# Decode attention with a gated MLP: two merged Wo transfers, a quartered x load, and the stores' semaphores

## The chip, the cores and the metric

The kernel runs on one core of a Trainium2 chip. The metric is the device time of one execution in microseconds (us); lower is better. "TensorE", "VectorE", "ScalarE", "GpSimd" and "SyncE" are the core's engines; the profile calls them PE (PEld for its weight loads), DVE, ACT, POOL and SP, and writes SPq or ACTq for what their instruction queues do, such as issuing transfers.

## The reference

One token for each of B = 8 sequences, D = 512. All tensors are bf16.

```python
xn = layernorm(x)                                   # [8, 512]
q  = xn @ wq                                        # 512 x 4096: 32 heads of 128
k, v = last 2048 of the 8192 cached positions       # 8 kv heads, each for 4 q heads
p  = softmax(q k^T * 128**-0.5);   o = p v          # [8, 4096]
s  = o @ wo                                         # 4096 x 512
g  = silu((sigmoid(xn @ w_gate) * (xn @ w_up)) @ w_down)   # 512 -> 1792 -> 512
out = x + s * g
```

## The kernel before

**What is loaded.** Every large tensor is read once: Wq as one transfer of 4 MB, the keys as 8 of 4 MB, the values as 16 of 2 MB, gate and up as two of 1.8 MB, down as one of 1.8 MB, and Wo (`wo_sb`) as eight pieces. All of these are issued by SyncE through `load` (L110 to L113) and so stand in one queue; each spreads over 128 partitions. x (`x_bf`, L122) is one transfer of 8 rows of 1 KB, issued by ScalarE.

**What sets the order.** `loads` (L194 to L202) is a list written ahead: keys and values by due times, then gate/up, the last two values, down, and Wo last of all. `issue_loads` (L208) issues from it as long as the buffer that the next load needs has been released: three buffers for Wq, keys and weights (`kring`), four for values (`vring`). The engines' instruction order is the order in which the program is written (`manual_schedule`, L88).

**What is computed.** LayerNorm of x on VectorE (L236 to L249), its transpose on TensorE (L259), the q projection on Wq (L391). Then one loop over 116 slots (L654): VectorE transposes keys in place (`k_turn`, L450), TensorE forms scores (L465), softmax follows, and TensorE multiplies the values (`pv`, L599, and `pv_sum`, L619). Gate and up (`unit_in`, L341) and down (`unit_out`, `b_ps`, L367) are placed among them. The last product is Wo:

```python
    for k in range(KW):          # KW = 32; row block k of Wo is wo_parts[k]
        for c in range(NCOL):    # two column halves, side by side on TensorE
            nc.tensor.matmul(a_ps[32*c : 32*(c+1), :], lhsT=o2_sb[:, k, :],
                             rhs=wo_parts[k][:, DC*c : DC*(c+1)], ...)
```

So `a_ps` (L702) takes the blocks k = 0 to 31 in order, and each block waits for the piece of Wo that holds it. A piece of blocks t0 to t1 is one run of (t1 - t0) KB on each of the 128 partitions. After `a_ps` come two VectorE instructions (`prod`, L713, and `y_bf`, L715) and the two stores (L717), one from SyncE and one from ScalarE.

**Semaphores of transfers.** The compiler layer gives the transfers eight completion semaphores in turn, in the order of the program. A transfer whose semaphore was used before waits, on the issuing engine, until the earlier user has landed. There are 39 transfers; the stores have semaphores 5 and 6 (counted from 0). At the end of the kernel (L746) SyncE waits for the semaphores in ascending order.

Of the kernel before, what the change touches and what calls it, by code (L numbers as in the profile page):

```python
# [10 lines left out]
def kernel(  # L11
# [13 lines left out]
    nc = tc.nc  # L25
    P = 128
# [83 lines left out]
    def load(dst, src, q=None):  # L110
        if q is None:
            q = nc.sync
        q.dma_start(out=dst, in_=src)  # L113

    def k_tile(shape, name):
        return kring.tile(shape, bf16, name=name, tag="kring", align_bytes=ALIGN)
# [2 lines left out]
        return vring.tile(shape, bf16, name=name, tag="vring", align_bytes=ALIGN)  # L119

    x_bf = work.tile([B, D], bf16, name="x_bf")
    nc.scalar.dma_start(out=x_bf[:], in_=A_x.flatten_outer_dims())  # L122

    wq_sb = k_tile([P, KT, Hq * Dh], "wq_sb")
    load(wq_sb[:], A_wq.rearrange("(p kt) n -> p kt n", kt=KT))
# [49 lines left out]
    def load_wo():  # L175
        t = k_tile([P, KW, D], "wo_sb")
        for t0, t1 in (
            (0, 8),
            (8, 16),
            (16, 20),  # L180
            (20, 24),
            (24, 28),
            (28, 30),
            (30, 31),
            (31, 32),
        ):
            load(t[:, t0:t1, :], wo_view[:, t0:t1, :])
            for k in range(t0, t1):
                wo_parts[k] = t[:, k, :]
# [18 lines left out]
    def issue_loads():  # L208
        while loads_done[0] < len(loads):
            x = loads[loads_done[0]]  # L210
            kind, i = x
            order, n = (v_order, VRING) if kind == 1 else (k_order, KRING)
            at = order.index(x)
            if at >= n and order[at - n] not in released:
                break
            if kind == 0:
                load_k(i)
            elif kind == 1:
                load_v(i)
            else:  # L220
                (load_gate_up, load_down, load_wo)[i]()
            loads_done[0] += 1
# [22 lines left out]
        out=rstd[:], in_=mv[:, 1:2], func=AF.Sqrt, bias=eps_t[:], scale=1.0  # L245
# [4 lines left out]
        out=xn_bf[:],  # L250
# [7 lines left out]
    for kt in range(KT):  # L258
        nc.tensor.transpose(  # L259
            out=xnT_ps[:, kt, :], in_=xn_bf[:B, kt::KT], identity=ident[:B, :B]  # L260
        )
    x2_ps = psum1.tile([NCOL * 32, DC], f32, name="x2_ps", tag="misc")
    for c in range(NCOL):
# [23 lines left out]
        out=PermF[:], in_=ident[:].rearrange("m (h q r) -> m q h r", q=NQ, r=rep)  # L287
# [4 lines left out]
        out=Hm[:],  # L292
        in_=ident[:].rearrange("p (a gl) -> p gl a", gl=GL),
# [6 lines left out]
    for j in range(GL):  # L300
        for gg in range(NG):
            g = NG * gg + j // 2
            nc.vector.tensor_copy(
                out=spread[:, gg, j % 2, :, j], in_=ident[:, 32 * g : 32 * g + PP]
# [5 lines left out]
        out=rows_of[:],  # L310
        in_=ident[:].rearrange("p (a m) -> p m a", m=w),
# [5 lines left out]
        out=Sel[:], in_=rows_of[:].rearrange("p (g c r) -> p c g r", g=GL, c=NCH)  # L317
# [5 lines left out]
    for gg in range(NG):  # L323
        rows = slice(32 * gg, 32 * (gg + 1))
        cols = slice(NE * GL * rep * gg, NE * GL * rep * (gg + 1))
        for e in range(NE):
            nc.vector.tensor_copy(
                out=pick[rows, e, cols].rearrange("p (h d) -> p h d", d=NE)[:, :, e],
                in_=ident[rows, 32 * gg : 32 * gg + GL * rep],
# [386 lines left out]
    for c in range(NCOL):  # L716
        queues[c].dma_start(  # L717
            out=out.flatten_outer_dims()[:, DC * c : DC * (c + 1)],
            in_=y_bf[32 * c : 32 * c + B, :],
# [31 lines left out]
```

## Time and profile before

| | us |
|---|---|
| median of 3 runs (197.93 to 197.95) | 197.94 |
| the profiled execution | 198.09 |
| its span, first to last instruction | 196.3 |
| PE / DVE / ACT busy in it | 90.5 / 109.9 / 27.4 |

The 40 digits of the profile's second part show the 16 transfer engines (its DMA row) at 9 tenths or more in every slice but the first and the last. The profile's fourth part follows the chain of work that ended last; its fifth and the timeline give instructions with the idle time before them and what ended that idle time.

### The profile page before, as it was taken

To read this page: it belongs to the slowest core of one execution; us is meant where nothing else is said; L and a number is where in the kernel's file an instruction comes from. 1 tells how busy PE (TensorE), PEld (TensorE's weight loads), DVE (VectorE), ACT (ScalarE), POOL (GpSimd) and SP (SyncE) were. 2 spreads that over 40 slices of the span, in tenths; PEclk is the share of its full clock that TensorE was granted. 3 is DMA by queue.
4 is the path that set the end of the run, shared out by engine and by line. 5 is a ranking of instruction groups with operands and counts; after the bars stand their busy time and mean duration, and the time that the engine had idled before them with its cause. 6 is when DMAs were issued, how large, how long until landed. Compare 5 with 4: busy or idle time off the path is not lost.

```text
span 196.3 us, 2503 instructions
## 1 busy us (share of the span) xinstructions
PE 90.5 (46%) x1046; PEld 43.9 (22%) x1046; DVE 109.9 (56%) x176; ACT 27.4 (14%) x69; POOL 1.6 (1%) x8
## 2 busy tenths in 40 slices
PE   0134004434333158403664764963566653555682
PEld 0011001111001012100332431342333331233561
DVE  3606399999999998899969836143000000120301
ACT  3006050000000074000000051420000004000000
POOL 3000000000000000000000000000000000000000
PEclk9999999999999999955558797599555555555879
DMA  6999999999999999999999999999999999999990
GB/s 235 447 441 434 441 429 441 427 434 424 434 427 427 427 427 434 417 424 451 441 414 431 427 427 427 429 431 431 427 431 427 434 430 435 424 426 423 422 363 19
DMA packets 5243, 81.18 MB, mean 414 GB/s; under 512 B 600, under 2 KB 880, under 8 KB 1392
## 3 DMA queue, kind: packets, MB, share of 16 engines
q1 hardware_dynamic: 5200, 81.01, 96.7%
q8 instruction: 8, 0.13, 0.2%
q10 hardware_dynamic: 32, 0.01, 0.0%
q14 instruction: 3, 0.02, 0.0%
HBM read 81.01 MB, written 0.01 MB: 413 GB/s over the span
## 4 chain that ended last, share of the span: by engine, by line
DMA 59%; DVE 27%; PE 9%; issue 1%; SPq 1%; ACT 0%; ACTq 0%; DVEq 0%
DVE k_sb L450 22%; DMA k_sb<-in_A_k_cache_dram 20%; DMA v_sb<-in_A_v_cache_dram 15%; DMA wgu_sb<-in_B_w_up_dram 13%; DMA wo_sb<-in_A_wo_dram 12%; PE pT_ps L526 3%; PE acc_ps L599 3%; PE s_ps L465 2%; DVE pT_sb L545 2%; DVE mx L479 1%; DVE pt_bf L513 1%; PE a_ps L702 1%; SPq L113 1%; PE den_ps L574 1%; PE o_ps L619 0%
## 5 line engine op out<-in xcount | busy, mean ns | idle before, releaser
L450 DVE STREAM_TRANSPOSE k_sb<-k_sb 128x1024 f32<-128x1024 f32 x64 | 73.9, 1208 | 5.7 <-DMA k_sb<-in_A_k_cache_dram 5.7
L465 PE MATMUL s_ps<-k_sb,qz_sb 128*32 128x512 bf16 x256 | 33.3, 585 | 56.5 <-DVE k_sb L450 50.7
L599 PE MATMUL acc_ps<-v_sb,pT_sb 128*32 128x256 bf16 x512 | 31.4, 367 | 17.4 <-DMA v_sb<-in_A_v_cache_dram 17.4
L628 DVE TENSOR_SCALAR o_sb<-o_ps,rden 16x128 bf16<-16x128 f32 x16 | 5.4, 336 | 46.3 <-PE o_ps L619 46.2
L465 PEld LDWEIGHTS <-qz_sb 128*32 128x32 bf16 x256 | 10.3, 121 | 73.8 <-issue 53.2
L599 PEld LDWEIGHTS <-pT_sb 128*32 128x32 bf16 x512 | 17.9, 121 | 28.9 <-DMA v_sb<-in_A_v_cache_dram 21.3
L610 ACT COPY acc_sb<-acc_ps 128x256 f32<-128x256 f32 x16 | 6.0, 373 | 81.1 <-PE acc_ps L599 81.1
L619 PE MATMUL o_ps<-acc_sb,Sel 128*16 128x128 f32 x64 | 14.1, 362 | 6.9 <-ACT acc_sb L610 6.9
L619 PEld LDWEIGHTS o_ps<-acc_sb,Sel 128*16 128x16 f32 x64 | 6.6, 118 | 13.9 <-ACT acc_sb L610 11.5
L526 PE MATMUL pT_ps<-pt_bf,spread 128*128 128x512 bf16 x16 | 7.5, 622 | 0.9 <-DVE pt_bf L513 0.7
L545 DVE TENSOR_SCALAR pT_sb<-pc_bf,Hm 128x1024 bf16<-128x1024 bf16 x16 | 6.6, 475 | 1.1 <-PE acc_ps L599 1.1
L391 PE MATMUL q_ps<-wq_sb,xnT_sb 128*32 128x512 bf16 x32 | 3.6, 629 | 7.5 <-DMA wq_sb<-in_A_wq_dram 7.5
L493 ACT ACT_TABLE_LOAD x1 | 1.3, 1283 | 39.4 <-DVE nm L487 39.4
L513 DVE STREAM_TRANSPOSE pt_bf<-p_bf 128x512 bf16<-128x512 bf16 x8 | 4.9, 674 | 2.2 <-ACT p_bf L493 2.2
L702 PE MATMUL a_ps<-wo_sb,o_sb 128*32 128x256 bf16 x64 | 5.7, 324 | 0.9 <-DMA wo_sb<-in_A_wo_dram 0.8
L534 ACT CAST pc_bf<-pT_ps 128x512 bf16<-128x512 f32 x8 | 4.6, 586 | 9.4 <-PE pT_ps L526 6.6
L422 ACT COPY qz_sb<-qT_sb 32x32 bf16<-32x32 bf16 x20 | 4.8, 241 | 7.7 <-DVE qT_sb L410 7.5
L479 DVE TENSOR_REDUCE mx<-s_ps 128x1 f32<-128x512 f32 x8 | 5.3, 659 | 1.0 <-PE acc_ps L599 1.0
L341 PE MATMUL d_ps<-wgu_sb,xnT_sb 128*32 128x448 bf16 x32 | 3.4, 573 | 4.9 <-DMA wgu_sb<-in_B_w_up_dram 2.5
L493 ACT ACTIVATE p_bf<-s_ps,nm 128x512 bf16<-128x512 f32 x8 | 5.4, 685 | 0.5 <-DVE nm L487 0.5
L410 DVE STREAM_TRANSPOSE qT_sb<-q_sb 128x512 bf16<-128x512 bf16 x2 | 1.4, 690 | 7.1 <-ACT q_sb L405 7.1
L702 PEld LDWEIGHTS <-o_sb 128*32 128x32 bf16 x64 | 4.4, 117 | 2.3 <-issue 1.9
(59 smaller groups left out, 37.2 us busy)
## 6 DMA issues: line engine op xcount, KB each, us to landing
k_sb<-in_A_k_cache_dram SPq DMA_DIRECT2D x8, 4096.0 KB, 21.8
v_sb<-in_A_v_cache_dram SPq DMA_DIRECT2D x16, 2048.0 KB, 18.5
wq_sb<-in_A_wq_dram SPq DMA_DIRECT2D x1, 4096.0 KB, 12.4
wo_sb<-in_A_wo_dram SPq DMA_DIRECT2D x2, 1024.0 KB
wgu_sb<-in_B_w_gate_dram SPq DMA_DIRECT2D x1, 1792.0 KB
wgu_sb<-in_B_w_up_dram SPq DMA_DIRECT2D x1, 1792.0 KB, 24.7
wd_sb<-in_B_w_down_dram SPq DMA_DIRECT2D x1, 1792.0 KB, 29.7
wo_sb<-in_A_wo_dram SPq DMA_DIRECT2D x3, 512.0 KB, 25.6
```

The source lines that it names most:

```text
L450: nc.vector.transpose(out=kw, in_=kw)
L465: nc.tensor.matmul(s_tiles[i][32 * g : 32 * (g + 1), :], lhsT=qz_sb[:, hb, h, 2 * a + e, :], rhs=kT[:, :, a, h, :, e], start=(n == 0), sto ...
L479: nc.vector.reduce_max(out=mx_of[hb][:, kq : kq + 1], in_=s_tiles[i][:], axis=AX.X)
L493: nc.scalar.activation(out=p_bf[:, :, kq], in_=s_tiles.pop(NK * hb + kq)[:].rearrange("p (o c j) -> p c j o", o=2, j=NC), func=AF.Exp, bia ...
L513: nc.vector.transpose(out=pt[:, w * n : w * (n + 1)], in_=p_bf[:, w * n : w * (n + 1)])
L526: nc.tensor.matmul(pT_ps[:], lhsT=spread[:, gg, y].rearrange("p k g -> p (k g)"), rhs=pt[:, c, y, :], start=(y == 0), stop=(y == 1), skip_ ...
L545: nc.vector.tensor_scalar(out=pT_of[hb, gg][:, :, gl, :], in0=pc, scalar1=Hm[:, gl : gl + 1], scalar2=None, op0=ALU.mult,)
L599: nc.tensor.matmul(acc_tiles[i][w * c : w * (c + 1), :], lhsT=pT[:, GL * rep * ch : GL * rep * ch + w], rhs=v_tiles[i][:, ch : ch + NCH, : ...
L610: nc.scalar.copy(out=acc_sb[:], in_=acc_tiles.pop(i)[:])
L619: nc.tensor.matmul(o_ps[rows, :], lhsT=Sel[:, c].rearrange("p g r -> p (g r)"), rhs=acc_sb[:, Dh * c : Dh * (c + 1)], start=(c == 0), stop ...
L628: nc.vector.tensor_scalar(out=o_sb[rows, b, :], in0=o_ps[rows, :], scalar1=rden_of[b // NQ][rows, b % NQ : b % NQ + 1], scalar2=None, op0= ...
L702: nc.tensor.matmul(a_ps[32 * c : 32 * (c + 1), :], lhsT=o2_sb[:, k, :], rhs=wo_parts[k][:, DC * c : DC * (c + 1)], start=(k == 0), stop=(k ...
```

## The change

The load of x becomes four transfers, one for each quarter of its columns (8 rows of 256 bytes each), still on ScalarE's queue. In Wo's list of pieces, blocks 0 to 16 become one transfer of 16 KB runs and blocks 16 to 24 one of 8 KB runs; the last four pieces (24 to 28, 28 to 30, 30 to 31, 31 to 32) are as before. There are then 40 transfers (three more for x, two fewer for Wo), and the stores come to semaphores 6 and 7, the last of the eight.

```diff
-    nc.scalar.dma_start(out=x_bf[:], in_=A_x.flatten_outer_dims())
+    for c in range(4):
+        nc.scalar.dma_start(
+            out=x_bf[:, P * c : P * (c + 1)],
+            in_=A_x.flatten_outer_dims()[:, P * c : P * (c + 1)],
+        )
...
     def load_wo():
         t = k_tile([P, KW, D], "wo_sb")
         for t0, t1 in (
-            (0, 8),
-            (8, 16),
-            (16, 20),
-            (20, 24),
+            (0, 16),
+            (16, 24),
             (24, 28),
             (28, 30),
             (30, 31),
```

No instruction of another engine is added, removed or moved. Waits move: the blocks 0 to 7 of `a_ps` now wait for the whole first half of Wo, and blocks 16 to 19 for the whole quarter 16 to 24. On SyncE, two issues of Wo go; each piece of Wo still waits for the transfer eight places before it, which for the last piece is now a value tile and was the down weights. Some key and value loads also wait for a quarter of x, whose semaphore they take over.

## The prediction

> **What bounds the kernel now.** I read the page first, for the transfer engines.
>
> ```profile
> DMA  6999999999999999999999999999999999999990
> GB/s 235 447 441 434 441 429 441 427 434 424 434 427 427 427 427 434 417 424 451 441 414 431 427 427 427 429 431 431 427 431 427 434 430 435 424 426 423 422 363 19
> DMA packets 5243, 81.18 MB, mean 414 GB/s; under 512 B 600, under 2 KB 880, under 8 KB 1392
> q1 hardware_dynamic: 5200, 81.01, 96.7%
> ```
>
> All 16 transfer engines are busy from the first slice to the last but one, with no dip. The 5200 packets of q1, SyncE's queue, are 36 loads of 128 rows plus 16 marks each, plus 16 for one store; the 600 below 512 bytes are 36 x 16 + 3 x 8, the marks of all 39 transfers. So a load costs each of the 16 engines eight rows and one mark. Next, SyncE's issues of loads:
>
> ```profile
> DMA to landing us min/median/max: 10.0/21.7/31.1
> L113 SPq DMA_DIRECT2D wo_sb<-in_A_wo_dram x8: 327/328/422, 153.5 to 182.6; - x8
> ```
>
> A load is issued at least 10.0 us before it lands: the queue always holds more work, and an issue or a wait on SyncE costs nothing until it is delayed by about that much. What counts is what the stream of loads has to move, and what comes after its last byte. That is in the chain of waits (start, duration, what) and in the timeline:
>
> ```profile
> 168.56 22.62 DMA wo_sb<-in_A_wo_dram
> 191.22 0.61 PE a_ps L702 x8
> 192.27 0.29 PE a_ps L702 x2
> 192.60 0.30 PE a_ps L702 x2
> 192.92 0.42 DVE prod L713
> 193.37 0.28 DVE y_bf L715
> ```
>
> ```profile
> 178.37 1.90 PE L599 MATMUL acc_ps<-v_sb,pT_sb 128*32 128x256 bf16 x32 [1.46 <-DMA v_sb<-in_A_v_cache_dram]
> 180.80 1.03 PE L619 MATMUL o_ps<-acc_sb,Sel 128*16 128x128 f32 x4 [0.54 <-ACT acc_sb L610]
> 184.22 2.25 PE L367 MATMUL b_ps<-wd_sb,hT_sb 128*32 128x256 bf16 x28 [1.36 <-DVE o_sb L649]
> 186.23 3.55 PE L702 MATMUL a_ps<-wo_sb,o_sb 128*32 128x256 bf16 x40
> 190.01 0.61 PE L702 MATMUL a_ps<-wo_sb,o_sb 128*32 128x256 bf16 x8 [0.24 <-DMA wo_sb<-in_A_wo_dram]
> 191.22 1.66 PE L702 MATMUL a_ps<-wo_sb,o_sb 128*32 128x256 bf16 x16 [0.60 <-DMA wo_sb<-in_A_wo_dram]
> ```
>
> TensorE takes blocks 0 to 19 of Wo (40 matmuls, two a block) without a stop, then waits for each later piece: blocks 24 to 27 land at about 191.2, the last at about 192.6, and the last pair ends at 192.90. The end is set by the landing of the last pieces, and the rest follows in fixed steps.
>
> **The change part by part.** *Fewer rows on the wire.* Windows of stages with different row lengths (their last number is GB/s):
>
> ```profile
> 30.00:80.00 50.00, 22.11 (x179) 6.78 (x168) 48.20 (x53) 6.41 (x13) 0.00 (x0) 1.00 1.00 432
> 120.00:160.00 40.00, 23.61 (x312) 12.16 (x312) 7.78 (x22) 5.22 (x12) 0.00 (x0) 0.63 1.01 430
> 181.00:186.00 5.00, 3.21 (x34) 2.42 (x34) 1.61 (x2) 0.00 (x0) 0.00 (x0) 0.84 1.01 426
> 186.00:189.00 3.00, 3.00 (x36) 2.62 (x32) 0.41 (x1) 0.38 (x1) 0.00 (x0) 0.56 1.01 408
> ```
>
> They are mostly rows of 32 KB, of 16 KB, of 8 KB, and of 4 KB with some of 8 KB. One engine moves a 32 KB row at 432/16 = 27.0 bytes/ns. An 8 KB row at 426/16 = 26.6 takes 308 ns against 303 at that rate; a 4 KB row at 408/16 = 25.5 takes 161 against 152. So a row costs 4 to 9 ns beyond its bytes. The change removes 256 rows, 16 on each engine, and two marks: 16 x 4 to 16 x 9 gives 0.06 to 0.14 us. I take 0.09, nearer the 8 KB window, which is the longer and purer of the two. It all lies ahead of the last landing: a gain of 0.09.
>
> The Trainium skill has a rule by which this would be much more: "DMA: Bandwidth & Descriptors", section "Anatomy of one DMA", gives each transfer a fixed cost of about 2.0 us besides its bytes. Two transfers fewer in the stream would then be an estimated 4 us less. The windows above contradict that for a full queue: the stream does not stop between transfers.
>
> *Issues and waits on SyncE.* Two issues of 0.33 us go, and each remaining piece waits for an earlier landing than before (the last for a value tile, not for the down weights). With a lead of 10.0 us, this is worth nothing, and nor are the waits on x's semaphores that some key loads gain: x has landed long before.
>
> *The first block waits longer.* Block 0 of `a_ps` now needs the whole first half. In the trace it started at 186.23. When did blocks 8 to 15 land? Blocks 20 to 23 landed just before 190.01; blocks 16 to 23 are 1.05 MB, at 408 GB/s 2.57 us, so the first half is there at 187.40, 187.35 with the gain above. TensorE starts the product 1.1 us later, and what hides that is its idle time before 190.01 and 191.22 (0.24 + 0.60) and its speed. A step of 256 columns takes (1.90 - 0.42)/7 = 0.211 us at granted clock 0.50 (the last values of 178.37: eight steps of four matmuls side by side), and (0.61 - 0.27)/3 = 0.113 at clock 1.00 (at 190.01), with the durations of the extremes here:
>
> ```profile
> L702 PE MATMUL a_ps<-wo_sb,o_sb x64: 269/273/421, 186.2 to 192.6; 128*32 128x256 bf16 x64
> ```
>
> 24 steps must be done by 191.1, when blocks 24 to 27 land: 3.75 us. At full clock they take 2.7, at half 5.1. Break-even: 0.211n + 0.113(24 - n) = 3.75 gives n = 10.6 steps, so the clock must be full by 187.35 + 10.6 x 0.211 = 189.6. Then the cost is nothing; otherwise the first rival holds.
>
> *x in four.* Rows from the start:
>
> ```profile
> L122 ACTq DMA_DIRECT2D x_bf<-in_A_x_dram x1: 581/581/581, 0.7 to 0.7; - x1
> 2.60 0.41 DVE L236 CAST x_f<-x_bf 8x512 f32<-8x512 bf16 x1 [2.60 <-DMA x_bf<-in_A_x_dram]
> 5.64 0.10 PEld L391 LDWEIGHTS <-xnT_sb 128*32 128x32 bf16 x1 [0.24 <-DVE xnT_sb L277]
> 13.17 3.60 PE L391 MATMUL q_ps<-wq_sb,xnT_sb 128*32 128x512 bf16 x32 [7.46 <-DMA wq_sb<-in_A_wq_dram]
> 22.79 2.37 DVE L450 STREAM_TRANSPOSE k_sb<-k_sb 128x1024 f32<-128x1024 f32 x2 [3.53 <-DMA k_sb<-in_A_k_cache_dram]
> ```
>
> Three more issues on ScalarE are 3 x 0.58 = 1.74 us; its table load and the square root stand behind them. VectorE's statistics and its constants stand behind the wait for x. If the quarters land promptly, x is there at 4.3 and the normalised x at 7.4, against Wq at 13.17: hidden by 5.8 us. If each of a quarter's row and mark waits behind a 32 KB row (1.2 us), six more packets add 7.3, and the product starts 1.5 us late; then the 3.53 us in which VectorE waits for the first keys cover it. On the stream itself six small packets more on each of eight engines cost 6 x 4 to 6 x 9 ns, 0.02 to 0.05 us, if one of these engines is the last to finish, and nothing otherwise; 0.02 taken. Nothing there can come out below zero.
>
> *The stores' semaphores.* The end in SyncE's rows:
>
> ```profile
> L746 SPq EVENT_SEMAPHORE x8: 17/28/28, 194.1 to 196.2; - x8
> SPq L746 <- DMA out_dram<-y_bf: 1.1, 2, 0.7
> ```
>
> SyncE goes through the semaphores in ascending order and really waits only for the two stores. With the stores on 5 and 6, one more wait stands behind the last store; on 6 and 7 none does. One such instruction lasts 28 ns; its dispatch may double that: 0.03 to 0.06, taken as 0.05.
>
> *Sum:* -0.09 + 0.02 - 0.05 = -0.12 us, for the profiled execution 198.09 to 197.97, and since that one was 0.15 above the median of 197.94, 197.82 on the runs' scale.
>
> **The rivals.** *Slower: the clock takes the place of the landing.* The granted clock (the number ahead of the last two) changes on a grid of 3.41 us; the first number after the length is PE's busy time:
>
> ```profile
> 140.85:144.26 3.41, 2.77 (x36) 1.39 (x28) 0.07 (x1) 0.37 (x1) 0.00 (x0) 0.50 1.00 428
> 144.26:147.67 3.41, 1.90 (x32) 1.08 (x32) 0.27 (x1) 0.12 (x1) 0.00 (x0) 0.50 1.01 432
> 178.39:181.81 3.42, 2.88 (x36) 1.52 (x37) 0.00 (x0) 0.37 (x1) 0.00 (x0) 0.50 1.00 428
> 181.81:185.22 3.41, 1.61 (x25) 1.42 (x26) 1.61 (x2) 0.00 (x0) 0.00 (x0) 1.00 1.00 420
> 185.22:188.63 3.41, 3.41 (x38) 2.93 (x34) 0.41 (x1) 0.38 (x1) 0.00 (x0) 0.50 1.01 412
> 188.63:192.05 3.42, 2.56 (x40) 1.99 (x37) 0.00 (x0) 0.00 (x0) 0.00 (x0) 1.00 0.75 283
> ```
>
> After a window at half clock with 2.77 us busy the next stays at half; after 2.88 or 3.41 it is full. Now the window 185.22 to 188.63 would hold `b_ps` until 186.48 (1.26) and `a_ps` from 187.35 (1.28): 2.54, under 2.77, so 188.63 to 192.05 stays at half. From 187.35 to 192.05 are 22 steps; the other ten at full clock take 1.13, and the last ends 0.27 - 0.11 later: 193.34, that is 0.44 after 192.90. With the 0.05 of the end: 198.33. If the clock never rose, 32 steps of 0.211 would end at 194.3, and the time would be near 199.3. Against it: this depends on 2.88 having just passed. The window opens at 178.39, 0.02 after `acc_ps` began; some tenths either way and it is under 2.77, `b_ps` runs its 14 steps at half clock for 3.0 us, to 187.2, no gap is left ahead of `a_ps`, and the next window is busy throughout, so the clock is full by 189.6 for most positions of the grid. Whether the grid stands still against the kernel from run to run no row shows. 15%.
>
> The Trainium skill, "TensorE: Matmul & The Clock Gate", section "Part 1: The HAM clock gate", calls the window of about 3.4 us free-running, not reset by a kernel's start. The length agrees with the six rows; that it is free-running no run here shows yet. Free running would make this rival an occasional run and not the median.
>
> *Slower: the start.* The added issues hold back the issue of Wq or its rows by one issue time, 0.58, and the whole stream moves: 198.4. For it: both queues issue at 0.73. Against: Wq is issued beside x's first quarter, as before. 4%.
>
> *Faster: all row costs go.* If the merged 3.1 MB came at 432 instead of 408 GB/s, 7.7 us would become 7.3: 0.43 less, with the end 197.46. For it: the last windows fall to 408. Against: the first two pieces already run at 426. 12%.
>
> *Nothing happens:* the last landing hangs on one engine that loses time elsewhere, and neither rows nor marks matter: 197.94. 9%. The forecast keeps 60%.
>
> **How the numbers follow.** 0.2%, or 0.4 us, is about what a measurement of this kernel can tell from no change. Forecast and "nothing" are within it (69%). Faster by more: the third rival, and 1% of the rest: 13%. Slower by more: the first rival, whose 0.39 lies at the bound, with later clocks beyond it, and the second, less 1% for clock cases within the bound: 18%. Time 197.82; range 197.55 to 198.35, which takes in the forecast's bounds (0.06 + 0.03 - 0.05 to 0.14 + 0.06) and the clock's nearest case.
>
> **What would show it.** Right: the first half's blocks wait at about 187.4, `a_ps` waits again before 191.2, the last pair ends at about 192.8, and one wait less follows the last store. Wrong: half clock in the window after 188.6, with `a_ps` running into the end unbroken; a first transpose of keys much after 22.8; or a last landing that moved by more than 0.2.

## The result and the profile after

The changed kernel takes 197.51 us (median of 22 runs, 197.28 to 197.95), the kernel before, run beside it, 197.89 (22 runs, 197.52 to 198.25). The ratio is 0.9987 with a 95% interval of 0.9981 to 0.9992: 0.26 us faster, between 0.16 and 0.38; the two medians lie 0.38 apart, at the end of that interval. A second comparison on another occasion gave 0.9989 (0.9981 to 0.9998), 0.22 us. The profiled execution is 197.41 us with a span of 195.6.

The page's rows on transfers:

```profile
DMA packets 5003, 81.18 MB, mean 415 GB/s; under 512 B 624, under 2 KB 896, under 8 KB 1152
q1 hardware_dynamic: 4912, 81.01, 97.0%
q10 hardware_dynamic: 80, 0.01, 0.0%
```

SyncE's queue has 288 packets fewer (256 rows and 32 marks), ScalarE's 48 more (three quarters of 8 rows and 8 marks): the change does what it says. The start, in the timeline:

```profile
0.73 1.79 ACTq L123 DMA_DIRECT2D x_bf<-in_A_x_dram  x4
13.02 0.41 DVE L238 CAST x_f<-x_bf 8x512 f32<-8x512 bf16 x1 [13.02 <-DMA x_bf<-in_A_x_dram]
16.05 3.60 PE L393 MATMUL q_ps<-wq_sb,xnT_sb 128*32 128x512 bf16 x32
22.60 2.37 DVE L452 STREAM_TRANSPOSE k_sb<-k_sb 128x1024 f32<-128x1024 f32 x2
```

x arrives at 13.0 us instead of 2.6. The q projection starts at 16.05 instead of 13.17, and the first transpose of keys begins without the 3.53 us of idle time that stood ahead of it. It begins at 22.60, where it was 22.79: the lateness used up the whole cover and cost nothing yet. The end, as the chain of waits and as TensorE's timeline:

```profile
190.98 0.61 PE a_ps L704 x8
191.62 0.59 PE a_ps L704 x6
192.24 0.30 PE a_ps L704 x2
192.57 0.42 DVE prod L715
184.42 3.17 PE L369 MATMUL b_ps<-wd_sb,hT_sb 128*32 128x256 bf16 x28 [1.36 <-DVE o_sb L651]
187.36 5.17 PE L704 MATMUL a_ps<-wo_sb,o_sb 128*32 128x256 bf16 x64
```

`a_ps` starts at 187.36, directly behind `b_ps`, catches up and again follows the landings: the last pair starts at 192.24, against 192.60. A second profile of the changed kernel shows the waits for the later pieces:

```profile
189.68 1.05 PE L704 MATMUL a_ps<-wo_sb,o_sb 128*32 128x256 bf16 x16 [0.52 <-DMA wo_sb<-in_A_wo_dram]
190.99 1.55 PE L704 MATMUL a_ps<-wo_sb,o_sb 128*32 128x256 bf16 x16 [0.26 <-DMA wo_sb<-in_A_wo_dram]
```

The windows of the clock's grid in the first profile (PE busy first, granted clock third from the end):

```profile
178.51:181.92 3.41, 2.58 (x36) 1.31 (x25) 0.26 (x1) 0.37 (x1) 0.00 (x0) 0.50 1.04 443
181.92:185.33 3.41, 1.92 (x14) 1.26 (x15) 1.35 (x2) 0.00 (x0) 0.00 (x0) 0.50 0.98 418
185.34:188.76 3.42, 3.42 (x36) 2.83 (x34) 0.41 (x1) 0.38 (x1) 0.00 (x0) 0.50 0.98 409
188.76:192.17 3.41, 3.25 (x52) 2.61 (x49) 0.00 (x0) 0.00 (x0) 0.00 (x0) 1.00 0.68 255
```

Here the first window holds 2.58 us, not 2.88; the next stays at half clock, `b_ps` takes 3.17, no gap is left, the third window is busy throughout and the clock is full from 188.76. That is the course that the prediction gave as the usual one.

SyncE's instructions from the last store's landing on (count, durations, first and last start), before and after:

```profile
L746 SPq EVENT_SEMAPHORE  x2: 28/28/28, 195.4 to 195.5; - x2
L746 SPq DRAIN  x2: 7/7/7, 195.5 to 195.6; - x2
```

```profile
L748 SPq EVENT_SEMAPHORE  x1: 28/28/28, 194.8 to 194.8; - x1
L748 SPq DRAIN  x1: 7/7/7, 194.9 to 194.9; - x1
```

Before, the wait that the store ends is followed by another; after, by none.

### The profile page after: what moved, and what is told of

Same layout as the page of the kernel before. It is cut to its first block, busy times and chain, and to the rows that moved or that the text cites. A ratio compares the mean times of both kernels' runs of the same rounds, so it can differ in the third digit from the quotient of the medians.

```text
span 195.6 us, 2508 instructions
## 1 busy us (share of the span) xinstructions
PE 90.8 (46%) x1046; PEld 44.3 (23%) x1046; DVE 110.2 (56%) x176; ACT 27.5 (14%) x69; POOL 1.6 (1%) x8
## 4 chain that ended last, share of the span: by engine, by line
DMA 55%; DVE 31%; PE 9%; issue 2%; ACTq 1%; ACT 0%; DVEq 0%
DMA v_sb<-in_A_v_cache_dram 25%; DVE k_sb L452 22%; DMA wo_sb<-in_A_wo_dram 16%; DMA k_sb<-in_A_k_cache_dram 9%; DMA x_bf<-in_A_x_dram 6%; PE pT_ps L528 3%; PE acc_ps L601 2%; PE s_ps L467 2%; DVE pT_sb L547 2%; DVE mx L481 1%; DVE pt_bf L515 1%; DVE qz_sb L422 1%; PE a_ps L704 1%; DVE qT_sb L412 1%; ACTq L123 1%
## 5 line engine op out<-in xcount | busy, mean ns | idle before, releaser
L601 PE MATMUL acc_ps<-v_sb,pT_sb 128*32 128x256 bf16 x512 | 31.9, 372 | 17.7 <-DMA v_sb<-in_A_v_cache_dram 17.7
L621 PEld LDWEIGHTS o_ps<-acc_sb,Sel 128*16 128x16 f32 x64 | 6.4, 116 | 13.9 <-ACT acc_sb L612 11.6
L528 PE MATMUL pT_ps<-pt_bf,spread 128*128 128x512 bf16 x16 | 6.9, 581 | 0.7 <-DVE pt_bf L515 0.7
L704 PE MATMUL a_ps<-wo_sb,o_sb 128*32 128x256 bf16 x64 | 5.0, 302 | 0.2
```

Source lines behind the costliest of these rows:

```text
L528: nc.tensor.matmul(pT_ps[:], lhsT=spread[:, gg, y].rearrange("p k g -> p (k g)"), rhs=pt[:, c, y, :], start=(y == 0), stop=(y == 1), skip_ ...
L601: nc.tensor.matmul(acc_tiles[i][w * c : w * (c + 1), :], lhsT=pT[:, GL * rep * ch : GL * rep * ch + w], rhs=v_tiles[i][:, ch : ch + NCH, : ...
L621: nc.tensor.matmul(o_ps[rows, :], lhsT=Sel[:, c].rearrange("p g r -> p (g r)"), rhs=acc_sb[:, Dh * c : Dh * (c + 1)], start=(c == 0), stop ...
L704: nc.tensor.matmul(a_ps[32 * c : 32 * (c + 1), :], lhsT=o2_sb[:, k, :], rhs=wo_parts[k][:, DC * c : DC * (c + 1)], start=(k == 0), stop=(k ...
```

## The experiments

All ratios are to the kernel before, run beside each variant; us are the ratio's distance from 1 times 197.9.

**Wo merged, x whole.**

```diff
             (0, 8) ... (20, 24)   ->   (0, 16), (16, 24)
```

> x stays one transfer, Wo's blocks 0 to 16 and 16 to 24 are merged: 37 transfers, the stores on semaphores 3 and 4 (three waits stand behind the last store, before it was one). Theory A (fewer rows and marks in the stream, and the number of waits behind the last store): -0.09 for the rows, +0.12 for two more waits of 0.06, so about +0.03 us against before, and in the profile three waits behind the last landing. Theory B (the gain came because ScalarE's program grew by three issues and so moved the 8 KB instruction refill away from the last store): nothing moves the refill here, so one instruction packet still falls beside the stores and the last store lands as late after its issue as before (1.7 us); the time is +0.03 as well, so the profile tells. Theory C (the stream's start differs from run to run): no change that can be told.

Measured: 1.0002 (0.9994 to 1.0011), +0.04 us. All three theories put the time there, so it does not choose between them. Four of SyncE's waits lie between the last landing and the drain, the one that the store ends and three more, as theory A has it:

```profile
L744 SPq EVENT_SEMAPHORE  x4: 28/28/28, 194.8 to 194.9; - x4
L744 SPq DRAIN  x1: 7/7/7, 195.0 to 195.0; - x1
```

An instruction packet does fall beside the stores, as theory B has it, but the last store landed 1.45 us after its issue and not 1.7. So the merge by itself, with the stores' place that it brings, gains nothing that can be told; by theory A, two more waits behind the store give back what the rows save.

**x in quarters, Wo as before.**

```diff
-    nc.scalar.dma_start(out=x_bf[:], ...)
+    # four loads of 128 columns each, as in the change
```

> x as four quarters, Wo as before: 42 transfers, the stores on semaphores 0 and 1 (four waits behind the last store). Theory A: +0.02 for x and +0.18 for three more waits, +0.20 us. Theory B: the refill moves away from the stores as in the changed kernel, -0.25, so about -0.05, with no instruction packet in the last 3 us. x lands at about 13 us as in the changed kernel, and the first transpose of keys begins within 0.3 us of the one before.

Measured: 1.0015 (1.0006 to 1.0024), +0.30 us (0.12 to 0.47). That is theory A's side, not B's: the instruction packet did move away from the stores, to 191.2 us, and the time did not fall. The first transpose of keys is as early as in the changed kernel:

```profile
22.59 2.37 DVE L453 STREAM_TRANSPOSE k_sb<-k_sb 128x1024 f32<-128x1024 f32 x2
```

**One spare load.**

```diff
+    for c in range(1):
+        spare = work.tile([B, D], bf16, name=f"spare{c}")
+        nc.scalar.dma_start(out=spare[:], in_=A_x.flatten_outer_dims())
```

> The kernel before with one more load of x into a buffer that nothing reads, issued by ScalarE behind x: 40 transfers, the stores on semaphores 6 and 7 as in the changed kernel, Wo and x as before. Theory A: one wait less, -0.05 us, and no wait behind the last store. Theory B: between 0 and -0.25, by where the refill falls with one more issue.

Measured: 0.9997 (0.9988 to 1.0006), -0.06 us: the value of theory A, though the interval (-0.24 to +0.12) holds nothing as well, and most of theory B's span.

**Wo merged, x in three.**

> Wo merged as in the change, x as three pieces (128, 128 and 256 columns): 39 transfers, the stores on semaphores 5 and 6 as before. Against the changed kernel only the semaphores differ, and one issue of x. Theory A: -0.07 us against before, 0.05 worse than the changed kernel. Theory B: -0.3, as the refill has moved, no worse than the changed kernel by more than 0.06. x lands at about 10.5 us.

Measured: 0.9994 (0.9985 to 1.0002), -0.12 us. The changed kernel, whose stores stand one place later, had -0.26 and -0.22; the interval (-0.30 to +0.04) holds the figures of both theories. x landed a quarter earlier than with four pieces:

```profile
10.78 0.41 DVE L237 CAST x_f<-x_bf 8x512 f32<-8x512 bf16 x1 [10.78 <-DMA x_bf<-in_A_x_dram]
```

**Wo's rows made shorter.**

```diff
             (0, 8) ... (20, 24)   ->   (0, 2), (2, 4), ... (22, 24)
```

> The other way round and larger: blocks 0 to 24 of Wo as twelve transfers of 2 KB runs instead of four of 8 and 4 KB; x whole; 47 transfers, so the stores stay on semaphores 5 and 6. Each transfer engine gets 96 rows there where it had 32, so 64 rows and eight marks more. At the 4 to 9 ns a row of the prediction: +0.26 to +0.58 us, marks with them +0.3 to +0.65. Theory A therefore expects 0.3 to 0.65 us slower, which would put the gain of the merge (16 rows, two marks fewer) at 0.07 to 0.15. Rival (rows cost nothing; the gain of the merge is noise of the start): no change beyond 0.1. Rival of the page's fixed cost per transfer (about 2 us each): +16 us.

Measured: 1.0017 (1.0009 to 1.0026), +0.34 us (0.18 to 0.51). With 64 rows and eight marks more on each engine that is 5.3 ns a row, marks included (2.8 to 8), so the merge's 16 rows, if they cost the same each, are worth 0.085 us (0.045 to 0.13). Neither rival's figure appeared.

**Wo's first three quarters as one transfer.**

```diff
             (0, 8) ... (20, 24)   ->   (0, 24)      x in quarters as in the change
```

> Merged further: blocks 0 to 24 of Wo as one transfer of 24 KB runs, x as four quarters: 39 transfers, the stores on semaphores 5 and 6. The first block can start only when block 23 has landed, at about 189.8 us instead of 187.4. Cover-gone theory: 24 blocks at 0.113 us (full clock) take 2.7 us to 192.5, at 0.211 (half) 5.1 us; with the eight blocks behind them the last ends at 193.4 at full clock and at up to 195.5 with the half clock that an idle TensorE would have: 0.6 to 2.8 us slower, at rows' gain of 0.13. Rival (the wait for the first half has a lot of cover still): within 0.2 us of the changed kernel.

Measured: 1.0126 (1.0109 to 1.0144), +2.5 us, in the range of the cover-gone theory. TensorE waits, its clock falls, and the product runs into the end unbroken:

```profile
189.87 5.34 PE L702 MATMUL a_ps<-wo_sb,o_sb 128*32 128x256 bf16 x64 [3.20 <-DMA wo_sb<-in_A_wo_dram]
187.11:190.52 3.41, 0.65 (x12) 0.65 (x13) 0.41 (x1) 0.00 (x0) 0.00 (x0) 1.00 0.90 360
190.52:193.93 3.41, 3.41 (x36) 2.95 (x33) 0.00 (x0) 0.00 (x0) 0.00 (x0) 0.50 0.20 72
193.93:197.35 3.42, 1.28 (x23) 0.99 (x18) 0.69 (x2) 0.00 (x0) 0.00 (x0) 1.00 0.01 2
```

The idle window at full clock (0.65 busy) is followed by one at half clock, in which 3.41 us of product get little done. So the cover of the longer first wait ends between the two: a wait for half of Wo costs nothing that can be told, one for three quarters does.

**Three spare loads.**

> The kernel before with three more loads of x into buffers that nothing reads, on ScalarE behind x: 42 transfers, the stores on semaphores 0 and 1, Wo and x as before. Against the one with a single spare load only the place of the stores among the waits changes by much: four waits stand behind the last store instead of none but its own pass. Theory A: 4 x 0.06 = 0.24 us slower than with one spare load, +0.18 against before; about the same as x in quarters alone, since x's lateness is covered. If instead x's lateness costs something, this one is faster than x in quarters alone by that much.

Measured: 1.0018 (1.0009 to 1.0027), +0.36 us, beside +0.30 for x in quarters with the stores on the same semaphores. x's lateness costs nothing that can be told. Both times are above the 0.18 expected, though the intervals (0.18 to 0.53 and 0.12 to 0.47) reach it.

Part of both times lies where no profile looks. Every run has its time and its span from the first to the last instruction. The time is longer by 1.79 to 1.83 us on average for the kernel before and for every variant but three: x in quarters (1.94), three spare loads (1.95) and x in eight (2.05). So 0.13 to 0.15 us of the +0.30 and +0.36 lie outside the span, and what they are stays open. The spans themselves are 0.12 and 0.21 longer on average than those of the kernel before, which is 0.04 to 0.07 for each of three more waits.

**x in eight.**

```diff
+    # eight loads of 64 columns each
```

> x as eight pieces of 64 columns, Wo as before: 46 transfers, the stores on semaphores 4 and 5 (two waits behind, +0.06). In the changed kernel row and mark of each quarter alternate with 32 KB rows, 2.44 us a quarter, and x lands at 12.9 us. Eight pieces: 2.0 + 7 x 2.44 + some 0.4 = 19.5 or, with the 10.8 us for three pieces carried on, 22.7 us. The chain from x to the q projection and the first transpose of keys took 9.6 us in the changed kernel, so the first transpose begins at 29 to 32 instead of 22.6. Theory (cover): VectorE is then 6 to 10 us late, and as it works without a pause from 26 to 100 us and releases the key buffers, the loads run dry for some us: 2 to 8 us slower. Rival (slack of the load queue takes it all): within 0.3 us.

Measured: 1.0184 (1.0168 to 1.0200), +3.6 us: in the range, and for a reason that none of the theories had. SyncE's wait and its first issues of keys, a window of the start (its last numbers are the transfer engines' share and GB/s), and the first transpose:

```profile
SPq L113 <- DMA wq_sb<-in_A_wq_dram: 12.2, 1, 12.2
13.38 7.94 SPq L113 DMA_DIRECT2D k_sb<-in_A_k_cache_dram  x3
10.00:14.00 4.00, 0.00 (x0) 0.00 (x0) 0.00 (x0) 0.00 (x0) 0.00 (x0) 1.00 0.45 190
26.35 2.37 DVE L453 STREAM_TRANSPOSE k_sb<-k_sb 128x1024 f32<-128x1024 f32 x2 [2.69 <-DMA k_sb<-in_A_k_cache_dram]
```

Eight pieces and Wq are more than the eight semaphores, and in the trace the first key load waits for the very semaphore that Wq was given. So it has to wait until Wq has landed: it is issued at 13.38 instead of 1.18, the stream falls to 190 GB/s, and everything behind comes some 3.6 us later. x itself is there at 14.1, not at 19.5 or later: no rows of the keys stood in its way. VectorE waits for the keys, not for x.

**Wo merged, x whole, three spare loads; and the changed kernel again.**

> Wo merged as in the change, x whole, and three spare loads of x behind it that nothing reads: 40 transfers, the stores on semaphores 6 and 7. It is the changed kernel without x's lateness (x should land at about 2.3 us instead of 12.9). Theory (x's lateness is covered, its gain is only the count of transfers): the same as the changed kernel within 0.1 us, -0.15 to -0.25 us against before. Rival (x's lateness costs some tenths): faster than the changed kernel by 0.1 to 0.3 us.

> The changed kernel again, beside the one with spare loads and on the same chip: -0.1 to -0.35 us against before, by the interval of its first comparison (0.9981 to 0.9992).

Measured: 0.9988 (0.9979 to 0.9996) and 0.9989 (0.9981 to 0.9998), -0.24 and -0.22 us. With x at 2.52 us instead of 13.02 the time is the same within the intervals (-0.42 to -0.08 and -0.38 to -0.04): beside the count of transfers, no effect of the quarters on the time shows.

```profile
2.52 0.41 DVE L237 CAST x_f<-x_bf 8x512 f32<-8x512 bf16 x1 [2.52 <-DMA x_bf<-in_A_x_dram]
```

**Four small fills on VectorE, alone and with the merge and spare loads.** By then the sum of rows and wait fell short of the measured gain, and the profiles offered a cause: an 8 KB instruction packet beside the stores, which the changed kernel has earlier.

```diff
+    fill = work.tile([B, 4], f32, name="fill")
+    for c in range(4):
+        nc.vector.memset(fill[:, c : c + 1], 0.0)
```

> The kernel before with four small fills of an unused tile on VectorE, in its idle time ahead of x; transfers, semaphores and waits as before. Theory D (the 8 KB instruction packet late in the run belongs to VectorE's program; in the changed kernel VectorE's wait for four semaphores of x adds two instructions to it, so that the packet comes at about 191 us and not at 194.5 to 195.0 beside the stores, where in three of six profiles the last store landed 0.3 us later): no instruction packet in the last 3 us, the last store lands 1.45 us after its issue, and the time is about 0.15 us below before. Rival (the packet costs nothing in most runs): within 0.05 us of before.

> Wo merged, x whole, three spare loads behind it (stores on semaphores 6 and 7), and the four small fills on VectorE: all that the changed kernel gains, without a late x. Theory A with D: -0.09 for the rows, -0.06 for the wait, -0.15 for the packet: -0.30 us, as the changed kernel. Theory A without D: -0.15 us.

Measured: 1.0002 (0.9993 to 1.0011) alone, +0.04 us, and 0.9997 (0.9988 to 1.0006) with the rest, -0.06. In the first, the transfers of the last 3 us are the two stores alone, without an instruction packet:

```profile
DMA packets 32, 0.01 MB, mean 3 GB/s; under 512 B 16, under 2 KB 32, under 8 KB 32
q10 hardware_dynamic: 16, 0.00, 0.8%
q1 hardware_dynamic: 16, 0.00, 0.7%
```

The packet is gone and the time has not moved: the interval (-0.14 to +0.22) leaves no room for the 0.15 of theory D, if only just. The second came out less good than the same kernel without the fills (-0.24), with overlapping intervals (-0.24 to +0.12 beside -0.42 to -0.08). Its profiled execution, 198.34 against the median of 197.78, shows something else:

```profile
178.44:181.85 3.41, 2.83 (x36) 1.53 (x36) 0.00 (x0) 0.37 (x1) 0.00 (x0) 0.50 1.05 449
181.85:185.26 3.41, 1.62 (x23) 1.38 (x24) 1.61 (x2) 0.00 (x0) 0.00 (x0) 1.00 0.96 411
185.26:188.67 3.41, 2.50 (x28) 1.84 (x24) 0.41 (x1) 0.38 (x1) 0.00 (x0) 0.50 0.98 411
188.68:192.09 3.41, 3.41 (x36) 2.82 (x34) 0.00 (x0) 0.00 (x0) 0.00 (x0) 0.50 0.75 287
187.59 5.85 PE L706 MATMUL a_ps<-wo_sb,o_sb 128*32 128x256 bf16 x64 [0.91 <-DMA wo_sb<-in_A_wo_dram]
```

This is the prediction's first rival, step by step: the first window with 2.83 us is followed by full clock, `b_ps` ends early, TensorE waits 0.91 us, the window with 2.50 is followed by half clock, and `a_ps` runs unbroken to 193.44. It is one execution, 0.56 us above its median.

## Why the prediction was right, and where it was short

**Direction and class.** Forecast: -0.12 us, within 0.2%. Measured: -0.26 (-0.38 to -0.16), 0.13%. The range was 197.55 to 198.35. The ratio applied to the 197.94 of the prediction's three runs gives 197.68, inside it; the bare 197.51, from runs in which the kernel before itself took 197.89, lies 0.04 below its end. The forecast's size was about half of what came.

**A sign of being wrong that appeared.** The prediction named a last landing that moves by more than 0.2; between the two profiles it moved by 0.36. Most of that is spread between executions. `prod`, which stands right behind the last pair, began at 192.60, 192.67, 192.70, 192.91 and 192.92 in the five profiles with Wo as before (x in eight, late as a whole, left out). It began at 192.54, 192.57, 192.58, 192.68 and 192.70 in five of the six with the two merged pieces; the sixth is the one with the fills. The means are 0.15 apart.

**Rows on the wire: right in kind, perhaps small.** 0.09 was taken, from 0.06 to 0.14; the amplified experiment gives 0.085 (0.045 to 0.13), the ten profiles 0.15 with a wide spread. By the fixed cost per transfer that the Trainium skill gives ("DMA: Bandwidth & Descriptors", section "Anatomy of one DMA"), twelve transfers in place of four would have cost 16 us; they cost 0.34. That section gives its figure for transfers that GpSimd issues, and no run here had one.

**The wait behind the last store: right.** 0.05 was taken; the profiles show one wait less, some 0.06 us. The two kernels with three more waits came out 0.30 and 0.36 slower, but inside the span only 0.12 and 0.21, which is 0.04 to 0.07 a wait. One wait less by itself (one spare load) is not clear of noise.

**What the sum lacks.** Rows and wait make 0.085 + 0.06 = 0.15, just below the first interval (0.16 to 0.38) and inside the second (0.04 to 0.38). With the 0.15 of the ten profiles for the rows they would make 0.21. Whether the rows' term was too small or something else gains a tenth stays open. The packet beside the stores and x's lateness show no sign of it, but intervals of 0.17 to either side would hide a tenth. The 0.02 that the prediction took for x's small packets is below what any run here can tell.

**The longer first wait: right, and safer than the profile of before made it look.** The break-even was full clock by 189.6. In four of the six profiles with the two merged pieces it came at 187.06 to 188.76, in a fifth at 189.68 without harm (`prod` at 192.68). In the profile of before, `a_ps` began at 186.23 because `b_ps` had the full clock. In three others with Wo as before, `b_ps` ran at half clock and `a_ps` began at 187.26, 187.26 and 187.56, about where the merge puts it. In the last, it began at 186.09, as `b_ps` itself had started 1.2 us sooner.

**The first rival: right in course and price, not in its bound.** It put the last pair's end at 193.34 and 0.44 us on the time; the execution that shows it has 193.44 and 0.56. One of six profiles is near the 15% that it was given. The prediction took it that a window at half clock with less than 2.77 us of busy time is followed by half clock. Two pairs of windows, one from the second profile of the changed kernel and one from x in quarters, show that it is no sharp bound:

```profile
183.65:187.06 3.41, 2.63 (x26) 2.14 (x27) 0.73 (x1) 0.00 (x0) 0.00 (x0) 0.50 0.93 394
187.06:190.47 3.41, 2.89 (x54) 2.67 (x51) 0.41 (x1) 0.38 (x1) 0.00 (x0) 1.00 0.99 395
123.02:126.43 3.41, 3.15 (x34) 1.33 (x36) 0.17 (x1) 1.92 (x4) 0.00 (x0) 0.50 1.01 432
126.43:129.84 3.41, 2.93 (x52) 1.88 (x44) 2.19 (x6) 0.37 (x1) 0.00 (x0) 0.50 0.99 423
```

2.63 is followed by full clock, 3.15 by half. Whether the grid stands still against the kernel was left open: it does not. The full clock begins at 188.76 in one profile of the changed kernel and at 187.06 in the other, and 1.70 is no multiple of 3.41. That agrees with the Trainium skill's word "free-running" ("TensorE: Matmul & The Clock Gate", section "Part 1: The HAM clock gate").

**The other rivals did not come.** The stream did not start later (the first keys were transposed at 22.60, not after 22.8). "All row costs go" asked for 0.48 us; the interval ends at 0.38, and the amplified experiment prices rows where the forecast did. "Nothing happens" asked for none; the interval begins at 0.16.

**x in four: right that it is hidden, with the extreme as the rule.** The prediction's worst case, a row or mark behind a 32 KB row each time, had x 7.3 us later than prompt, at 11.6; it was 13.0. The later packets did follow each other at the 1.2 us that it took, but the second quarter's rows did not move before 5.95 us, though the first quarter was through at 2.2. The cover named for that case, VectorE's 3.53 us before the keys, was used up to nothing.

## What to carry to other kernels

Where transfers are the bound and their queue is always full, as here, neither issues nor the number of transfers counted, only bytes, a few nanoseconds a row, and what stands behind the last landing; at a fixed count of semaphores, look at which of them the last stores get, and whether an early load has to wait for the one it takes over. A small load that shared the engines with rows of 32 KB was best issued whole: each further piece waited for about two such rows. When a wait is moved in front of TensorE, count its steps at both clocks, and expect the clock to differ from one execution to the next.

## What the runs showed of the hardware

In the changed kernel's trace the rows and the marks of x's second, third and last quarter pass in turn, some 1.2 us apart: rows from 5.95, marks from 7.18, rows from 8.39, and so on to the last marks at 12.05 to 12.54. A 32 KB row takes 1.2 us at 27 bytes/ns, so these times fit one such row between a quarter's rows and its marks, and one between its marks and the next rows. A quarter more put x's landing off by 2.24 us (10.78 with three pieces, 13.02 with four).

The completion semaphores are a resource of the stream: with eight of them, seven more small loads ahead of the keys made the first key load wait 12.2 us, and the transfer engines fell to a share of 0.45.

The busy time of a window, as the profile counts it, does not give a sharp threshold for the clock. At half clock, windows of 3.41 us with 2.63, 2.83 and 2.88 us busy were followed by full clock, and windows with 2.58, 2.77 and 3.15 by half.
